# Instructions in the engines' main bodies instead of a block

## Chip, core and metric

The kernel runs on one core of a Trainium2 chip. The metric is the device time of one execution in microseconds; the time of a kernel is the median of several executions. A core has five engines, each with its own instruction stream: TensorE (PE; its weight loads are listed apart as PEld), VectorE (DVE), ScalarE (ACT), GpSimd (POOL) and SyncE (SP). [...] In the profile, a "q" behind an engine's name means its sequencer: the part that waits, jumps, drains and issues transfers.

## The reference

`x` is (1, 2048, 512) in bf16. A token mixer with a residual is followed by an MLP with a residual:

```python
def reference(x, w1, w2, w3, w4):
    h = _gelu(_layernorm(x, axis=-1) @ w1)
    ...                       # four quarters of h, shifted by 1, -1, 2, -2 tokens: g0..g3
    hs = jnp.concatenate([g0, g1, g2, g3], axis=-1) @ w2
    x1 = x + hs
    h2 = _gelu(_layernorm(x1, axis=-1) @ w3) @ w4
    return x1 + h2
```

`w1` and `w2` are 512 x 512, `w3` is 512 x 1792 and `w4` is 1792 x 512.

## The kernel before

The kernel describes its work as a list of operations, each with its engine, what it reads and what it writes. A small scheduler puts them into one order (`prog.seq`). Then `emit` writes them, with the needed waits, into the engines' instruction streams. The operations that the text speaks of:

```python
# loads of x: SyncE, and half of tile 0 on ScalarE        (lines 292, 296)
yield pg.add(eng, f"dma_x{t0}",
             lambda e: e.dma_start(x_sb[:, t0:t1, :], xt[:, t0:t1, :]), ...)
# zeros on VectorE, and matmuls on them that warm TensorE  (lines 269, 535)
pg.add("dve", "zeros", lambda e: e.memset(zeros[:], 0.0), ...)
ins = e.matmul(o_ps[:, b, :], zeros[:, 0:P], zeros[:], start=True, stop=True)
# the last stage: matmul with w4, add x1, store            (lines 511, 519, 522)
ins = e.matmul(dst, h2T[:, fc, P * t : P * (t + 1)], w4_sb[:, fc, cs], ...)
pg.add("dve", f"res{t}_{hh}", ... e.tensor_tensor(o_sb[:, oi, c], d, x1_sb[:, t, c], ALU.add) ...)
pg.add("sp", f"out_dma{t}_{hh}", ... e.dma_start(outt[:, t, c], o_sb[:, oi, c]) ...)
```

`emit` opens a block, notes the body that the block has for each engine, and writes each operation into that body. Behind the last operation SyncE waits for all 18 output transfers:

```python
    with nc.Block() as block:                                # line 593
        bodies = {}
        def keep(name):
            def _body(e):
                bodies[name] = nc.cur_body
            return _body
        block.gpsimd(keep("pool"))
        block.sync(keep("sp"))
        ...                                                  # scalar, vector, tensor
        for op in prog.seq:
            ...                                              # which semaphores it needs
            with nc.body(bodies[e]):
                ...
                engs[e].wait_ge(sems[s], v)                  # line 635
                ...
                ins = op.fn(engs[e])
                ins.then_inc(sems[op.stream], inc)
            ...
        with nc.body(bodies["sp"]):
            for op in prog.seq:
                if op.name.startswith("out_dma"):
                    nc.sync.wait_ge(sems[op.stream], 16)     # line 655
```

A program of this kind begins in a main body, which holds a few constants and one all-engine barrier (line 669 in the profile). From there each engine jumps to its own body of the block. At the block's end each engine jumps to a common end, where it drains and goes through a second all-engine barrier. In such a barrier each engine drains and adds to a semaphore, GpSimd collects four of these and adds to a second semaphore, and each engine waits for that one.

Of the kernel before, what the change touches and what calls it, by code (L numbers as in the profile page):

```python
# [12 lines left out]
ENGINES = ["sp", "act", "pe", "dve", "pool"]  # L13
# [191 lines left out]
def bass_standalone__mixer_s_mlp__prompt_kernel(nc, x, w1, w2, w3, w4, out):  # L205
# [14 lines left out]
    with ExitStack() as es:  # L220
# [356 lines left out]
        pg.line(queue)  # L577
        pg.order()
        emit(nc, es, pg)

def emit(nc, es, prog):

    engs = {"sp": nc.sync, "act": nc.scalar, "pe": nc.tensor, "dve": nc.vector, "pool": nc.gpsimd}
    sems = {e: es.enter_context(nc.semaphore("sem_" + e)) for e in ENGINES}
    ndma = 0
    for op in prog.seq:
        if op.queue is not None:
            op.stream = ("dma", ndma)
            sems[op.stream] = es.enter_context(nc.semaphore(f"sem_dma{ndma}"))
            ndma += 1  # L590
        else:
            op.stream = op.eng
    with nc.Block() as block:
        bodies = {}

        def keep(name):
            def _body(e):
                bodies[name] = nc.cur_body

            return _body  # L600

        block.gpsimd(keep("pool"))
        block.sync(keep("sp"))
        block.scalar(keep("act"))
        block.vector(keep("dve"))
        block.tensor(keep("pe"))
        know = {e: {} for e in ENGINES}
        implied = {}
        count = {}
        last_write, readers = {}, {}  # L610
        for op in prog.seq:
            e = op.eng
            needs = {}

            def need(sv):
                if needs.get(sv[0], 0) < sv[1]:
                    needs[sv[0]] = sv[1]

            for res, ver in op.reads:
                lw = last_write[res]  # L620
                assert lw[2] == ver, (op.name, res, ver, lw)
                need(lw)
            for res, ver in op.writes:
                if res in last_write:
                    need(last_write[res])
                for sv in readers.get(res, ()):
                    need(sv)
            if e == "pe":
                needs.pop("pe", None)
            k = know[e]  # L630
            with nc.body(bodies[e]):
                for s, v in sorted(needs.items(), key=lambda sv: -sv[1]):
                    if k.get(s, 0) >= v:
                        continue
                    engs[e].wait_ge(sems[s], v)
                    for s2, v2 in implied[(s, v)].items():
                        if v2 > k.get(s2, 0):
                            k[s2] = v2
                    k[s] = max(k.get(s, 0), v)
                ins = op.fn(engs[e])  # L640
                inc = 1 if op.queue is None else 16
                ins.then_inc(sems[op.stream], inc)
            val = count[op.stream] = count.get(op.stream, 0) + inc
            snap = dict(k)
            snap[op.stream] = max(snap.get(op.stream, 0), val)
            implied[(op.stream, val)] = snap
            for res, ver in op.reads:
                readers.setdefault(res, []).append((op.stream, val))
            for res, ver in op.writes:
                last_write[res] = (op.stream, val, ver)  # L650
                readers[res] = []
        with nc.body(bodies["sp"]):
            for op in prog.seq:
                if op.name.startswith("out_dma"):
                    nc.sync.wait_ge(sems[op.stream], 16)


# [26 lines left out]
```

## Time and profile before

| | |
|---|---|
| three timed executions | 139.0, 139.03 and 138.16 us, median 139.0 |
| profiled execution | 137.98 us |
| span, first to last instruction | 136.1 us |
| granted TensorE clock | 1.00 |
| instructions on record | 2007 |

The span is what the records of one execution cover, from the first instruction to the last; the device time is somewhat longer. The profile's parts that matter here are the table of busy times, the chain of work that ended last (followed back from the end, at each step to what released it), and the rows of single source lines, with the sequencers' instructions. Busy time counts only an engine's own work, so jumps, drains and barriers have to be looked for in the rows of the lines that made them: 669 for the main body, 593 for the block, 655 for the waits for outputs.

### The profile page before, as it was taken

The numbers are of one execution on the slowest core, as the hardware profiler recorded it, in microseconds if no ns is written. First come the engines' busy times: TensorE is split into PE (matmuls) and PEld (weight loads), VectorE is DVE, ScalarE is ACT, GpSimd is POOL, SyncE is SP. The second block draws the span as 40 slices with busy tenths as digits, with TensorE's granted clock in tenths as the row PEclk, the third lists the DMA queues.
The fourth block names the chain that finished last, engine by engine and source line by source line (L and its number), as shares of the span: only waits on it lengthen the run. The fifth ranks groups of instructions, "written<-read, shape, count | busy, mean of one in ns | idle before, by whom it ended". The sixth has DMA issues, their size and how long they took to land.

```text
span 136.1 us, 2007 instructions
## 1 busy us (share of the span) xinstructions
PE 130.8 (96%) x787; PEld 73.4 (54%) x800; DVE 59.0 (43%) x170; ACT 51.3 (38%) x70; POOL 19.4 (14%) x43
## 2 busy tenths in 40 slices
PE   6799999999999999999999999999999999999993
PEld 2287788776668644444444444444444444444472
DVE  1888899998899640043610053210002222322231
ACT  4899657444566455530066630036660000000000
POOL 2441483333043310001010010000000000000000
PEclk9999999999999999999999999999999999999999
DMA  3999975574379551001210003110000111111121
GB/s 104 279 371 406 357 236 102 106 90 79 70 206 174 99 113 39 0 0 39 82 39 0 0 0 76 39 39 5 0 0 30 47 39 39 43 39 39 40 72 45
DMA packets 21401, 12.19 MB, mean 90 GB/s; under 512 B 13840, under 2 KB 20880, under 8 KB 21392
## 3 DMA queue, kind: packets, MB, share of 16 engines
q1 hardware_dynamic: 21248, 12.00, 33.4%
q8 instruction: 6, 0.10, 0.3%
q10 hardware_dynamic: 144, 0.07, 0.2%
q14 instruction: 3, 0.02, 0.1%
HBM read 6.82 MB, written 2.10 MB: 65 GB/s over the span
## 4 chain that ended last, share of the span: by engine, by line
PE 85%; DVE 5%; POOL 3%; DMA 2%; issue 1%; SPq 1%; ACT 0%
PE y_ps L442 40%; PE o_ps L511 35%; PE o_ps L482 9%; POOL rstd L366 3%; DMA x_sb<-in_x_dram 2%; DVE xn_buf L372 1%; DVE st L349 1%; PE y_ps L415 1%; DVE x_sb L493 1%; POOL xn_buf L383 1%; SPq L296 1%; DVE x_sb L489 1%; DVE mv L351 0%; DVE st6b L343 0%; DVE vpe L355 0%
## 5 line engine op out<-in xcount | busy, mean ns | idle before, releaser
L442 PE MATMUL y_ps<-xnT,w_sb 128*128 128x256 bf16 (+2 forms) x435 | 64.1, 305 | 0.3
L442 PEld LDWEIGHTS y_ps<-xnT,w_sb 128*128 128x128 bf16 x440 | 40.4, 98 | 23.7 <-issue 0.4
L511 PE MATMUL o_ps<-w_sb,h2T 128*128 128x512 bf16 (+2 forms) x250 | 48.8, 355 | 0.1
L457 ACT ACTIVATE h2T<-y_ps 128x1024 bf16<-128x1024 f32 (+1 forms) x29 | 28.6, 993 | 36.6 <-PE y_ps L442 36.6
L511 PEld LDWEIGHTS o_ps<-w_sb,h2T 128*128 128x128 bf16 x252 | 23.6, 98 | 25.2
L519 DVE TENSOR_TENSOR o_sb<-o_ps,x_sb 128x512 bf16<-128x512 f32 (+2 forms) x18 | 11.4, 632 | 44.3 <-PE o_ps L511 44.1
L366 POOL TENSOR_TENSOR rstd<-vpe,neghalf 128x1 f32<-128x1 f32 x31 | 16.9, 557 | 61.6 <-DVE vpe L355 49.6
L493 DVE TENSOR_TENSOR x_sb<-o_ps,x_sb 128x512 bf16<-128x512 f32 x14 | 9.6, 689 | 22.2 <-PE o_ps L482 22.2
L349 DVE BATCH_NORM_STATS2 st<-x_sb 128x6 f32<-128x512 bf16 x26 | 17.5, 684 | 2.2 <-DMA x_sb<-in_x_dram 2.0
L482 PE MATMUL o_ps<-w_sb,hT 128*128 128x512 bf16 x58 | 15.0, 379 | 0.3
L372 DVE TENSOR_SCALAR xn_buf<-x_sb,mv,rstd 128x512 bf16<-128x512 bf16 x25 | 10.2, 411 | 3.8 <-POOL rstd L366 2.8
L457 ACT ACTIVATE hT<-y_ps 128x1024 bf16<-128x1024 f32 (+1 forms) x10 | 8.4, 850 | 7.7 <-PE y_ps L442 7.6
L482 PEld LDWEIGHTS o_ps<-w_sb,hT 128*128 128x128 bf16 x64 | 6.1, 98 | 5.3
L535 PE MATMUL o_ps<-zeros 128*128 128x512 bf16 x12 | 4.3, 534 | 1.2 <-DVE zeros L269 1.2
L380 ACT ACTIVATE xn_buf<-x_sb,nmr,rstd 128x512 bf16<-128x512 bf16 x5 | 4.0, 809 | 2.6 <-DVE nmr L376 2.6
L351 DVE BATCH_NORM_AGGREGATE mv<-st 128x2 f32<-128x6 f32 x26 | 4.1, 173 | 0.2
L355 DVE TENSOR_SCALAR vpe<-mv 128x1 f32<-128x1 f32 x26 | 3.5, 148 | 0.3
L324 ACT ACTIVATE junk<-x_sb 128x512 bf16<-128x512 bf16 x5 | 3.1, 628 | 0.7 <-DVE x_sb L489 0.7
L535 PEld LDWEIGHTS o_ps<-zeros 128*128 128x128 bf16 x12 | 1.5, 131 | 3.5 <-issue 2.1
L415 PE MATMUL y_ps<-ident,xn_buf 128*128 128x128 bf16 x28 | 2.4, 220 | 1.0 <-DVE xn_buf L372 0.9
L415 PEld LDWEIGHTS y_ps<-ident,xn_buf 128*128 128x128 bf16 x28 | 1.8, 98 | 2.1 <-DVE xn_buf L372 1.6
L420 ACT ACTIVATE xnT<-y_ps 128x512 bf16<-128x512 bf16 (+1 forms) x5 | 2.6, 548 | 0.1
(33 smaller groups left out, 18.8 us busy)
## 6 DMA issues: line engine op xcount, KB each, us to landing
out_dram<-o_sb SPq DMA_DIRECT2D x15, 128.0 KB, 1.7
w_sb<-in_w_dram SPq DMA_DIRECT2D x1, 1792.0 KB, 9.8
w_sb<-in_w_dram SPq DMA_DIRECT2D x2, 896.0 KB, 9.4
x_sb<-in_x_dram SPq DMA_DIRECT2D x2, 512.0 KB, 11.2
x_sb<-in_x_dram SPq DMA_DIRECT2D x2, 256.0 KB, 4.4
w_sb<-in_w_dram SPq DMA_DIRECT2D x2, 256.0 KB, 3.7
w_sb<-in_w_dram SPq DMA_DIRECT2D x1, 512.0 KB, 5.5
x_sb<-in_x_dram SPq DMA_DIRECT2D x3, 128.0 KB, 2.4
```

The costliest lines, as they stand in the source:

```text
L349: pg.add("dve", f"bnst{q}", lambda e: e.bn_stats(st6[:, q, :], src), reads=rs, writes=[(("st6", q), 0)], dur=605)
L351: pg.add("dve", f"bnag{q}", lambda e: e.bn_aggr(mv[:, q, :], st6[:, q, :]), reads=[(("st6", q), 0)], writes=[(("mv", q), 0)], dur=75)
L366: lambda e: e.tensor_tensor(col(rstd), col(vpe), neghalf[:], ALU.pow),
L372: lambda e: e.tensor_scalar(dst, src, mv[:, q, 0:1], rstd[:, q : q + 1], ALU.subtract, ALU.mult),
L415: ins = e.transpose(chunk(c), xn_buf[:, slot(q), P * c : P * (c + 1)], ident[:])
L442: ins = e.matmul(y_ps[:, p, W * i : W * (i + 1)], wsb[:, dc, P * fc : P * (fc + 1)], src[:, dc, P * t0 : P * t0 + W], start=(dc == 0), sto ...
L457: (lambda d, s: (lambda e: e.activation(d, s, ACT_F.Gelu_apprx_tanh)))(dst, ysrc),
L482: ins = e.matmul(dst, hT[:, j, c0 : c0 + P], w2_sb[:, j, :], start=(j == 0), stop=(j == DC - 1))
L493: f = lambda e: e.tensor_tensor(x1_sb[:, t, :], dst, x_sb[:, t, :], ALU.add)
L511: ins = e.matmul(dst, h2T[:, fc, P * t : P * (t + 1)], w4_sb[:, fc, cs], start=(fc == 0), stop=(fc == FC - 1))
L519: (lambda d, c: (lambda e: e.tensor_tensor(o_sb[:, oi, c], d, x1_sb[:, t, c], ALU.add)))(dst, cs),
L535: ins = e.matmul(o_ps[:, b, :], zeros[:, 0:P], zeros[:], start=True, stop=True)
```

## The change

The block goes. The operations are written straight into the main body, into each engine's stream, directly behind the barrier that the main body has anyway. So there is no jump into a block, none out of it, and no drain and barrier at its end. Operations, their order and their semaphores are the same; the rest of the diff is indentation.

```diff
-    with nc.Block() as block:
-        bodies = {}
-
-        def keep(name):
-            def _body(e):
-                bodies[name] = nc.cur_body
-
-            return _body
-
-        block.gpsimd(keep("pool"))
-        block.sync(keep("sp"))
-        block.scalar(keep("act"))
-        block.vector(keep("dve"))
-        block.tensor(keep("pe"))
-        know = {e: {} for e in ENGINES}
+    know = {e: {} for e in ENGINES}
 ...
-            with nc.body(bodies[e]):
-                for s, v in sorted(needs.items(), key=lambda sv: -sv[1]):
 ...
-                    engs[e].wait_ge(sems[s], v)
 ...
-                ins = op.fn(engs[e])
-                inc = 1 if op.queue is None else 16
-                ins.then_inc(sems[op.stream], inc)
+        for s, v in sorted(needs.items(), key=lambda sv: -sv[1]):
 ...
+            engs[e].wait_ge(sems[s], v)
 ...
+        ins = op.fn(engs[e])
+        inc = 1 if op.queue is None else 16
+        ins.then_inc(sems[op.stream], inc)
 ...
-        with nc.body(bodies["sp"]):
-            for op in prog.seq:
-                if op.name.startswith("out_dma"):
-                    nc.sync.wait_ge(sems[op.stream], 16)
+    for op in prog.seq:
+        if op.name.startswith("out_dma"):
+            nc.sync.wait_ge(sems[op.stream], 16)
```

More of the change, by code (lines that the diff above doesn't have):

```diff
@@ L592, in emit @@
             op.stream = op.eng
-    with nc.Block() as block:
-        bodies = {}
-        def keep(name):
-            def _body(e):
-                bodies[name] = nc.cur_body
-            return _body
-        block.gpsimd(keep("pool"))
-        block.sync(keep("sp"))
-        block.scalar(keep("act"))
-        block.vector(keep("dve"))
-        block.tensor(keep("pe"))
-        know = {e: {} for e in ENGINES}
-        implied = {}
-        count = {}
-        last_write, readers = {}, {}
-        for op in prog.seq:
[L612 to L630, printed above, removed]
-            with nc.body(bodies[e]):
-                for s, v in sorted(needs.items(), key=lambda sv: -sv[1]):
-                    if k.get(s, 0) >= v:
-                        continue
-                    engs[e].wait_ge(sems[s], v)
[L636 to L639, printed above, removed]
-                ins = op.fn(engs[e])
-                inc = 1 if op.queue is None else 16
-                ins.then_inc(sems[op.stream], inc)
[L643 to L651, printed above, removed]
-        with nc.body(bodies["sp"]):
-            for op in prog.seq:
-                if op.name.startswith("out_dma"):
-                    nc.sync.wait_ge(sems[op.stream], 16)
@@ new lines, in emit, with need @@
+    know = {e: {} for e in ENGINES}
+    implied = {}
+    count = {}
+    last_write, readers = {}, {}
+    for op in prog.seq:
+        e = op.eng
+        needs = {}
+        def need(sv):
+            if needs.get(sv[0], 0) < sv[1]:
+                needs[sv[0]] = sv[1]
+        for res, ver in op.reads:
+            lw = last_write[res]
+            assert lw[2] == ver, (op.name, res, ver, lw)
+            need(lw)
+        for res, ver in op.writes:
+            if res in last_write:
+                need(last_write[res])
+            for sv in readers.get(res, ()):
+                need(sv)
+        if e == "pe":
+            needs.pop("pe", None)
+        k = know[e]
+        for s, v in sorted(needs.items(), key=lambda sv: -sv[1]):
+            if k.get(s, 0) >= v:
+                continue
+            engs[e].wait_ge(sems[s], v)
+            for s2, v2 in implied[(s, v)].items():
+                if v2 > k.get(s2, 0):
+                    k[s2] = v2
+            k[s] = max(k.get(s, 0), v)
+        ins = op.fn(engs[e])
+        inc = 1 if op.queue is None else 16
+        ins.then_inc(sems[op.stream], inc)
+        val = count[op.stream] = count.get(op.stream, 0) + inc
+        snap = dict(k)
+        snap[op.stream] = max(snap.get(op.stream, 0), val)
+        implied[(op.stream, val)] = snap
+        for res, ver in op.reads:
+            readers.setdefault(res, []).append((op.stream, val))
+        for res, ver in op.writes:
+            last_write[res] = (op.stream, val, ver)
+            readers[res] = []
@@ L659 @@
+    for op in prog.seq:
+        if op.name.startswith("out_dma"):
+            nc.sync.wait_ge(sems[op.stream], 16)
 _INS = ['x', 'w1', 'w2', 'w3', 'w4']
```

## The prediction

> **What bounds the kernel now.** I read the busy table first, then the chain of waits, then the two ends of the run, because the change touches nothing but the two ends.
>
> ```profile
> PE 130.8 (96%) x787; PEld 73.4 (54%) x800; DVE 59.0 (43%) x170; ACT 51.3 (38%) x70; POOL 19.4 (14%) x43
> PE 85%; DVE 5%; POOL 3%; DMA 2%; issue 1%; SPq 1%; ACT 0%
> ```
>
> The first line is each engine's busy time, the second the shares of the chain that ended last. TensorE is busy for 130.8 of 136.1 us, and the chain lies on it for 85% of the span. A table of windows that I took over the span puts 125.40 us of that into the 126.25 us from 7.75 to 134.00 us. So the middle has no hole that a few instructions fewer could close. What is left is the head (0 to 7.75 us) and the tail (134.0 to 136.1 us).
>
> The head, from the chain in order of time (start, length, what held it):
>
> ```profile
> 0.65 0.07 issue
> 0.72 0.40 SPq L296
> 1.12 0.07 issue
> 1.19 0.42 SPq L296
> 1.61 0.05 issue
> 1.66 2.82 DMA x_sb<-in_x_dram
> ```
>
> SyncE leaves the first all-engine barrier at 0.65 us and issues its first load at 0.72; the next loads follow at 1.19 and 1.66, and the chain runs on through the transfer that is under way until 4.48 us. In this head the jump to SyncE's own block must lie within the 0.07 us between 0.65 and 0.72. The very next step, from one load to another with no jump in it, also takes 0.07 us. That is the first thing to see: the entry jump is nearly free here.
>
> The tail, first from the chain, in the window from 125 us on:
>
> ```profile
> 124.91 8.93 PE o_ps L511 x69
> 133.85 0.02 issue
> 133.87 0.29 DVE o_sb L519
> ```
>
> The last matmul ends at 133.85 and the last addition, which adds the residual, at 134.16 us. The chain counts computation only, so everything behind 134.16 has to be taken from the sequencers' own records. Line 655 is the loop in which SyncE waits for the output transfers; line 593 is the block itself, that is, what is behind its end. Columns: operation, count, shortest/median/longest ns, first and last start in us.
>
> ```profile
> L655 SPq EVENT_SEMAPHORE  x9: 17/28/28, 134.6 to 135.7; - x9
> ```
>
> ```profile
> L593 POOLq EVENT_SEMAPHORE  x2: 17/17/17, 136.0 to 136.0; - x2
> ...
> L593 PEldq DRAIN  x1: 1033/1033/1033, 132.8 to 132.8; - x1
> L593 DVEq DRAIN  x1: 330/330/330, 133.9 to 133.9; - x1
> L593 SPq COMPARE_BRANCH  x1: 33/33/33, 135.8 to 135.8; - x1
> L593 SPq DRAIN  x1: 13/13/13, 135.9 to 135.9; - x1
> L593 SPq EVENT_SEMAPHORE  x1: 17/17/17, 136.1 to 136.1; - x1
> ...
> L593 PEldq EVENT_SEMAPHORE  x1: 51/51/51, 136.1 to 136.1; - x1
> ```
>
> The other engines had reached the end long before (TensorE's drain starts at 132.8, VectorE's at 133.9). They wait at the barrier for SyncE, which waits for the last output transfer. From 135.7 to the end of the span at 136.1 us nothing is done but jump, drain and barrier.
>
> [...] The trace has only one jump on record at all, SyncE's at the end, with 33 ns, and 130 ns pass between it and the next instruction; for the other engines' jumps and for all five entry jumps it has none[...]. [...] the profiled execution took 137.98 us for a span of 136.14, so 1.84 us lie outside the records.
>
> **The change, part by part.** Compared engine by engine, both programs have the same work in the same order with the same waits; each engine loses four instructions (GpSimd five): a jump in, a jump out, a drain, and one wait on the barrier's semaphore (two semaphore operations on GpSimd, which collects and releases). The barrier ahead of the work stays. So there are three terms.
>
> 1. The entry jumps. SyncE's step from barrier to first load is 0.07 us, as is its step from load to load. ScalarE goes from the end of its barrier wait to its own load in 56 ns by the records. Nothing there has the size of a further stop. VectorE takes 172 ns to its memset of the zeros, and a jump may be in that; but the memset only starts the warm-up matmuls, and their row (L535) ends near 5.5 us, while TensorE's first transpose waits until 6.34 us for normalised data from the loads. On the path: 0.00 to 0.05 us; I take 0.02.
>
> 2. The exit on SyncE, the only one on the path. The records in nanoseconds: last wait for an output ends at 135.716; 37 to the jump's start; 33 for the jump; 130 until the drain; 13 for it; 25 until GpSimd sees it; 17 + 62 + 17 for GpSimd's two operations; 36 until the last engine reads the release; 51 for TensorE's operation on it. The sum is 421 ns and reaches the end of the span, 136.137. All of it goes: 0.42 us.
>
> 3. The waits for the outputs. There are 18 semaphores. Before, nine operations of line 655 take 17 and the jump carries the eighteenth; after, nine operations carry two each. The first eight start 0.06 us apart, at 134.57 to 135.01 us, all behind the last issue (134.19 to 134.52) and all ahead of the landing of that last transfer at 135.69, for which the ninth waits. So the repacking is hidden by 0.65 us: 0.00 us.
>
> Sum: 0.42 + 0.02 = 0.44 us of 136.14, that is 0.3%. The new span should be 135.7 us. The 1.84 us outside the records I leave as they are, minus perhaps 0.1 us, since four engines now come early to whatever stands behind the kernel; I chose this share, nothing shows it.
>
> **The rivals.**
>
> First, the **barrier's time is not saved but moved**[...]. For this speaks that SyncE comes last in any case and the last landing at 135.69 us doesn't move. [...] the time would stay at that of before, 138.5 to 139.0 us, with a shorter span.
>
> Second, the **entry jumps cost more than I see**[...]. Were all of it on the path, another 0.1 us would come off. The chain says otherwise: it goes over SyncE's loads, and neither memset nor warm-up is in it.
>
> Third, a **shifted start changes the transfers**: loads that start 0.02 us earlier could meet in another order in the queues, and TensorE at 96% busy would feel only a missed due time in the first 8 us. I see no cause for more than 0.1 or 0.2 us either way, as all loads move together.
>
> Fourth, **the scatter hides it all**: the three timed runs of before are 139.0, 139.03 and 138.16 us, and the profiled one 137.98. The gap between the two pairs, some 0.9 us, is twice the expected gain. A median of few runs can land on either.
>
> **Range and chances.** The median of before, 139.0, less 0.45 gives 138.55; the mean of all four executions, 138.54, less 0.45 gives 138.1. I choose 138.3 between the two. The range takes half a microsecond and a little more on each side for the scatter: 137.98 less 0.45 is 137.5 as the low end, and 139.0, the old median with no gain at all, as the high end. Faster by over 2% would need 2.8 us, more than the whole tail of 2.3 us behind the last matmul; slower by 2% would need an unforeseen stall of as much. So 0.02 and 0.01, and 0.97 for within 2%.
>
> **What would show it right or wrong.** Right: the rows of the block's end (drain, jump, barrier) are gone; the last record is SyncE's ninth wait for outputs; the span is 135.6 to 135.8 us; SyncE's first load starts 0.07 us behind the barrier as before; the chain's shares are the same. Step 1 is wrong if the first load or the memset of the zeros moves by more than 0.05 us and the first transpose with it. Step 2 is wrong if the tail from the last addition to the end doesn't shrink from 1.98 to about 1.55 us. The share outside the records is wrong if execution less span is no longer near 1.8 us. The prediction as a whole is wrong if the middle changes: another busy time of TensorE, or a granted clock below the 1.00 of now.

## The result and the profile after

Six executions of the changed kernel have a median of 137.27 us (136.93 to 138.08); six of the kernel before, beside them, have 138.93 us (138.09 to 139.30). The ratio is 0.9898, with a 95% interval of 0.9856 to 0.9941. So it is faster by about 1%, within the 2% to which the prediction gave 0.97, but by more than the predicted 0.3%; 137.27 also lies 0.2 us below the low end of the range, 137.5.

The profiled execution took 137.32 us for a span of 135.99 us. The page's busy table and the engine shares of the chain:

```profile
PE 131.5 (97%) x787; PEld 73.6 (54%) x800; DVE 58.9 (43%) x170; ACT 51.3 (38%) x70; POOL 19.4 (14%) x43
PE 85%; DVE 5%; POOL 3%; DMA 2%; issue 1%; SPq 1%; ACT 0%
```

The same work and the same chain, then, at the same granted clock of 1.00. The 0.7 us more on TensorE are the twelve warm-up matmuls (4.3 us before, 5.0 after), which are not on the chain: one takes 0.63 us at first and 0.38 at the end, and the short ones start at 4.45 us before and at 5.83 after. The head of the chain after (start, length, what held it):

```profile
0.66 0.07 issue
0.72 0.40 SPq L296
1.12 0.06 issue
1.18 0.43 SPq L296
1.61 0.05 issue
1.66 3.10 DMA x_sb<-in_x_dram
```

SyncE's first load still starts at 0.72 us. Its step from the barrier to the load is 68 ns in both kernels by the records, and VectorE's to its memset 172 before and 171 after: the entry jumps cost these two nothing. What differs is the transfer: 3.10 us instead of 2.82. The copy below takes up whether that is the block's doing. The end of the chain, and SyncE's waits for the outputs (now line 639):

```profile
124.98 9.15 PE o_ps L511 x70
134.13 0.02 issue
134.16 0.29 DVE o_sb L519
```

```profile
L639 SPq EVENT_SEMAPHORE  x9: 28/28/28, 134.9 to 136.0; - x9
```

The ninth wait, which starts at 135.96 and ends at 135.987 us, is the last record. Nothing stands on the block's line any more. Laid side by side from the records, in ns:

| stretch | before | after |
|---|---|---|
| start to second half of tile 0's statistics (needs the chain's load) | 4501 | 4785 |
| from there to the end of the last addition | 129661 | 129660 |
| last addition to the end of the span | 1975 | 1542 |
| device time less span (us) | 1.84 | 1.33 |

The middle is the same to a nanosecond. The tail lost 0.43 us, as predicted; the later load in this one execution gave 0.28 of it back, so the span fell by only 0.15 us. And the part outside the records fell by 0.51 us. That last row was not foreseen, and the experiments are about it.

### The profile page after: what moved, and what is told of

Its sections match the earlier page's. It is cut to its first block, busy times and chain, and to the rows that moved or that the text cites. A ratio compares the mean times of both kernels' runs of the same rounds, so it can differ in the third digit from the quotient of the medians.

```text
span 136.0 us, 1995 instructions
## 1 busy us (share of the span) xinstructions
PE 131.5 (97%) x787; PEld 73.6 (54%) x800; DVE 58.9 (43%) x170; ACT 51.3 (38%) x70; POOL 19.4 (14%) x43
## 4 chain that ended last, share of the span: by engine, by line
PE 85%; DVE 5%; POOL 3%; DMA 2%; issue 1%; SPq 1%; ACT 0%
PE y_ps L442 40%; PE o_ps L511 36%; PE o_ps L482 9%; POOL rstd L366 3%; DMA x_sb<-in_x_dram 2%; DVE xn_buf L372 1%; DVE st L349 1%; PE y_ps L415 1%; DVE x_sb L493 1%; POOL xn_buf L383 1%; SPq L296 1%; DVE x_sb L489 1%; DVE mv L351 0%; DVE st6b L343 0%; DVE vpe L355 0%
## 5 line engine op out<-in xcount | busy, mean ns | idle before, releaser
L535 PE MATMUL o_ps<-zeros 128*128 128x512 bf16 x12 | 5.0, 606 | 1.2 <-DVE zeros L269 1.2
```

## Experiments

Each kernel was timed beside the kernel before on the same chip. For each the time outside the records is given: device time less span, as the median of the 9 to 22 executions of that experiment. It holds what lies ahead of the first record together with what lies behind the last, and nothing here divides the two; differences between kernels are put down to the end, as the part ahead of the work is the same. It scatters by only +-0.07 us, far less than the times themselves, and +-0.05 of that is rounding, since the spans of these executions are on record to 0.1 us. The one profiled execution of each kernel, with a span to the nanosecond, gives the same values within 0.04 us. In the kernel before it was 1.82 or 1.83 us on every chip (27 to 57 executions).

### The changed kernel once more

> The changed kernel once more, unchanged. In the first profiles the tail behind the last addition shrank by 0.43 us and the time outside the records (device time less span) from 1.84 to 1.33, together 0.94 us or a ratio of 0.993; the measured ratio was 0.990. Theory of scatter (the first load of x lands at another time in each execution, and the rest is chance): spans from 135.5 to 137 us, outside 1.33 +- 0.05 in each execution, and a ratio that comes nearer to 0.993. Rival (the head is systematically faster without the block): the ratio stays at 0.990 or below, and the first tile's loads land earlier than in the kernel before.

Median 137.77 us against 138.29, ratio 0.9945 (0.9923 to 0.9967). Outside 1.37 us (mean 1.355), so 0.46 less than before. Together with the 0.42 us of jump, drain and barrier this makes 0.88 us, 0.64% of 138.3, a ratio of 0.9936; that lies within the intervals of both comparisons. The shortest executions agree: 137.17 against 138.04, 0.87 us. The ratio moved towards the sum, as the theory of scatter had it, and the head is not faster (second half of tile 0's statistics at 4.82 us). Nor is it slower as a rule, though the profiles alone could suggest it: those statistics start at 4.50 us in before and 4.62 in the other kernel below that keeps the block, and at 4.63 to 5.12 in the twelve without it. But the lower group of spans lies around 136.3 us for before and around 135.9 for the copy, 0.4 us apart, which is the exit alone. This profile also scatters in another place than I had put it: its middle is 130.45 us, not 129.66. That is taken up after the experiments.

### The barrier alone

> The changed kernel with one all-engine barrier put back behind the last wait, without block and jump. By the records of before, jump and the step behind it were 0.20 us of the tail, drain and barrier 0.22. Theory of late arrival (each engine has something to finish behind its last instruction, and the barrier lets four engines begin with it only when the last transfer has landed): tail 1.75 to 1.8 us, outside back at 1.8, so some 0.7 us above the changed kernel. Rival [...]: outside stays at 1.33, time 0.2 us above the changed kernel.

```diff
+    nc.all_engine_barrier()          # behind the last wait, in the main body
```

Rows of that line (operation, count, shortest/median/longest ns, first and last start):

```profile
L640 POOLq EVENT_SEMAPHORE  x2: 17/17/17, 136.8 to 136.9; - x2
L640 POOLq DRAIN  x1: 651/651/651, 82.3 to 82.3; - x1
...
L640 SPq DRAIN  x1: 7/7/7, 136.8 to 136.8; - x1
...
L640 PEldq EVENT_SEMAPHORE  x1: 51/51/51, 137.0 to 137.0; - x1
```

Median 138.24 us, ratio 0.9994 (0.9969 to 1.002), by the two ratios 0.68 us above the changed kernel, where 0.7 was expected; outside 1.83 us. From the last wait to the end of the span 0.25 us, where the kernel before had 0.42. So the barrier alone brings the whole time outside back, and 0.25 of the 0.42 us; the jump with the step behind it is the other 0.17. The rival, that the jump costs the time outside, is out. GpSimd's drain at 82.3 us shows that the engine had finished long ago and was only held by the barrier.

### All engines late, without a barrier

> The changed kernel, with one wait added at the end of each of the other four engines, for the last output transfer: no barrier, no drain, no jump, but all five engines reach their end together. Theory of late arrival: outside goes back to about 1.8 us, span as in the changed kernel (at most 0.05 more), time 0.5 us above it. Rival (barrier, drain or jump themselves cost the time outside): outside 1.33, time as the changed kernel.

```diff
+    last = [op for op in prog.seq if op.name.startswith("out_dma")][-1]
+    for e in ("act", "pe", "dve", "pool"):
+        engs[e].wait_ge(sems[last.stream], 16)
```

```profile
L642 ACTq EVENT_SEMAPHORE  x1: 17/17/17, 135.9 to 135.9; - x1
L642 POOLq EVENT_SEMAPHORE  x1: 17/17/17, 135.9 to 135.9; - x1
L642 DVEq EVENT_SEMAPHORE  x1: 21/21/21, 135.9 to 135.9; - x1
L642 PEldq EVENT_SEMAPHORE  x1: 51/51/51, 135.9 to 135.9; - x1
```

No drain, no barrier and no jump, yet outside is 1.86 us (ratio 0.9986, 0.9968 to 1.0004). So the time outside comes not from those instructions, but from engines that reach their end late.

### One engine late at a time

In these four the 18 waits for the outputs are moved to one other engine, and SyncE ends at its last issue:

```diff
-            nc.sync.wait_ge(sems[op.stream], 16)
+            engs["pool"].wait_ge(sems[op.stream], 16)     # or "act", "dve", "pe"
```

> The changed kernel with the 18 waits for the outputs on GpSimd instead of SyncE, so SyncE ends at its last issue and GpSimd is the only late engine. Theory of late arrival: the time outside is what the late engine has to finish, so it differs from 1.33 by the difference between the two engines, up or down by 0.1 to 0.5 us. Rival (time outside belongs to barrier or jump): 1.33 as in the changed kernel.

> The changed kernel with the 18 waits for outputs on ScalarE instead of SyncE. So far the time outside the records is 1.82 us in before, 1.36 with SyncE late alone, 1.86 with all five late, 2.12 with GpSimd late alone. Theory (each engine has its own finishing work, and the end waits for all of it; GpSimd's is the longest): ScalarE between 1.2 and 1.9 us. Rival (the engines finish in a fixed order, a chain that passes from one to the next; the earlier the late engine stands in it, the longer): also between these, but the five engines give five different, evenly spaced values.

> The changed kernel with the 18 waits on VectorE. Theory of own finishing work: outside 1.2 to 1.9 us. Rival of a fixed order: a value evenly spaced between those of the other engines. If any engine comes below SyncE's 1.36 at the same span, the waits belong on that engine and the kernel beats the changed one by the difference.

> The changed kernel with the 18 waits on TensorE. TensorE's semaphore operations take 51 ns in the records where SyncE's take 17 to 28, so the span may be 0.03 us longer. Theory of own finishing work: outside 1.2 to 1.9 us. Rival of a fixed order: evenly spaced values.

| engine that is late alone | outside, us | ratio (95%) |
|---|---|---|
| SyncE (changed kernel, the copy) | 1.37 | 0.9945 (0.9923 to 0.9967) |
| VectorE | 1.42 | 0.9944 (0.9916 to 0.9972) |
| ScalarE | 1.47 | 0.993 (0.9901 to 0.9959) |
| TensorE | 1.57 | 0.9949 (0.9925 to 0.9972) |
| GpSimd | 2.12 | 1.001 (0.9987 to 1.0033) |

The time outside depends on which engine is late, and for GpSimd it is the longest by far. The values are not evenly spaced (0.05, 0.05, 0.10, 0.55; the last is 0.33 with GpSimd's 1.90 for a single wait, below), so a fixed chain with equal steps doesn't fit. A chain with unequal steps, which passes from engine to engine, is not ruled out: it too would give each late engine a value of its own. GpSimd late alone, with all the waits on it, takes away the whole gain. No engine comes below SyncE: the changed kernel already waits on the cheapest one. The differences in time between the first four are smaller than their intervals; only the time outside tells them apart.

### GpSimd beside SyncE, GpSimd left out, GpSimd with one wait

> The changed kernel (SyncE waits for all outputs) with one wait for the last output on GpSimd as well. With all five late the time outside was 1.86 us, with GpSimd late alone 2.12. Theory (GpSimd's finishing work sets the end, and its nine operations at the end made it worse alone): 1.85 to 1.9 us here, which is the value of before, so GpSimd alone explains the whole 0.46 us. Rival (it takes several late engines to get 1.86): between 1.36 and 1.8. Third (a late GpSimd is worse when the others are early): 2.1.

> All five engines late gave 1.86 us outside the records, GpSimd with SyncE 1.90; ScalarE, VectorE and TensorE late alone gave 1.47, 1.42 and 1.57. Here all but GpSimd wait for the last output. Theory (the slowest of the late engines sets the time outside, and that is GpSimd): without it TensorE sets it, 1.5 to 1.6 us. Rival (it is the number of late engines): about 1.75, between one late and five.

> GpSimd late alone gave 2.12 us, but it then had nine operations with 18 waits at its end; with SyncE late too, and one wait on GpSimd, it was 1.90. Here SyncE waits for the first 17 outputs and GpSimd only for the last. Theory (the longer list of waits on GpSimd costs the 0.22 us): 1.90 us. Rival (a late GpSimd is worse when SyncE is early): 2.1 us.

```diff
 # pool_late_too: SyncE's waits stay
+    nc.gpsimd.wait_ge(sems[last.stream], 16)
 # four_late: as all engines late, but with: for e in ("act", "pe", "dve")
 # pool_last_only: SyncE waits for outs[:-1], and then
+    nc.gpsimd.wait_ge(sems[outs[-1].stream], 16)
```

Outside: 1.90 us with GpSimd late beside SyncE, 1.61 with the four others late and GpSimd early, 1.90 with one wait on GpSimd and SyncE early. The ratios are 0.9959 (0.9937 to 0.9981), 0.9959 (0.9944 to 0.9974) and 0.9994 (0.9974 to 1.0013). The first and the third are alike outside and still lie 0.0035 apart, so the scatter of the times hides what tells the three apart. The late engine with the largest value sets the time, not their number: without GpSimd it is near TensorE's 1.57. A chain with unequal steps would do the same. And of GpSimd's 2.12, 0.22 us belonged to its nine operations of waits:

```profile
L639 POOLq EVENT_SEMAPHORE  x9: 43/43/43, 119.0 to 136.5; - x9
```

```profile
L640 POOLq EVENT_SEMAPHORE  x1: 17/17/17, 136.8 to 136.8; - x1
```

The first line is of the kernel with all waits on GpSimd, the second of the one with the last alone. Why nine operations, eight of which were over before, cost 0.22 us behind the ninth stays open.

### The block's barrier in its other form

> The kernel before, with the block's closing barrier in its other form, without GpSimd's drain and with semaphores alone. GpSimd still leaves last, behind the landing of the last output. Theory of the late GpSimd: outside 1.8 to 1.9 us as in before, and at most the 0.25 us of the barrier change in the tail. Rival (the drain on GpSimd is what costs outside the records): outside 1.4 us.

```diff
-    with nc.Block() as block:
+    with nc.Block(no_gpsimd_drain=True) as block:
```

Outside 1.81 us, ratio 1.0021 (0.9992 to 1.005). So GpSimd's drain is not what costs the time outside, and this form gains nothing: GpSimd still ends only behind the last landing. The other four engines still drain in it, and SyncE's exit takes 0.49 us instead of 0.42, with one semaphore operation more.

This gives one number for six kernels. GpSimd's last record ends before the span does, by 0.087 us in before (136.050 against 136.137), 0.09 in the barrier alone and in this one, 0.04 with all late and 0.00 in the two with a single wait on GpSimd. Added to the time outside of 1.82, 1.83, 1.81, 1.86, 1.90 and 1.90, it comes to 1.90 to 1.92 us each time from GpSimd's last record to the end of the execution, with what lies ahead of the first record counted in.

### The last wait alone on SyncE

> On GpSimd nine operations of waits at the end instead of one cost 0.22 us outside the records (2.12 against 1.90). SyncE, the engine whose late end is the cheapest, carries such a list in the changed kernel. Here ScalarE waits for the first 17 outputs, which land 0.7 us earlier, and SyncE for the last alone. Theory (the list costs any engine the same): outside 1.1 to 1.2 instead of 1.36, and a kernel 0.2 us below the changed one. Rival (the list matters on GpSimd alone): 1.36, time as the changed kernel.

```diff
-    for op in prog.seq:
-        if op.name.startswith("out_dma"):
-            nc.sync.wait_ge(sems[op.stream], 16)
+    outs = [op for op in prog.seq if op.name.startswith("out_dma")]
+    for op in outs[:-1]:
+        nc.scalar.wait_ge(sems[op.stream], 16)
+    nc.sync.wait_ge(sems[outs[-1].stream], 16)
```

Outside 1.34 us, ratio 0.9941 (0.9918 to 0.9964): no gain that can be measured. The list of waits matters on GpSimd and not on SyncE, and the theory falls. No kernel that I tried is measurably faster than the changed one.

### Where the scatter is

From the second half of tile 0's statistics to the end of the last addition, the fourteen profiles fall into groups: 129.66 us in five (before and after among them), 130.30 to 130.50 in eight (the copy among them), 130.03 in one. The transposing transfers, line 389, in after and then in the copy:

```profile
L389 SPq DMA_TRANSPOSE xnT<-xn_buf x24: 1190/1264/1852, 19.2 to 82.6; - x24
```

```profile
L389 SPq DMA_TRANSPOSE xnT<-xn_buf x24: 1189/1265/2322, 19.3 to 83.5; - x24
```

In the copy one of them, issued at 27.2 us, held SyncE for 2.32 instead of 1.27 us. TensorE waits not for that one but for the one issued before it, at 25.86 us, which takes 4.12 us to land (most take 2.5). From the chain and from the waits of the copy:

```profile
25.86 4.12 DMA xnT<-xn_buf
29.98 0.14 issue
30.12 1.91 PE y_ps L442 x16
```

```profile
PE y_ps L442 <- DMA xnT<-xn_buf: 0.6, 1, 0.6
```

After's chain stays on TensorE from 19.98 us throughout that stretch. What goes with it is a 16 KB transfer on queue q8, whose kind the profile gives as instruction. It starts at 26.6 to 27.2 us in all eight profiles of the long kind, at 29.1 to 29.9 in the five short ones, and at 31.4 in the one between, which has its long transpose issue at 30.7. In both kinds it falls upon a transposed transfer; what differs is which. In the copy it starts 1.08 us behind the issue at 25.86, whose transfer TensorE soon needs, and is still under way when SyncE issues the next. In after it starts 1.07 us behind the issue at 28.38. That transfer lands late too, after 3.6 us, but the next issue comes only at 30.53 us and keeps its 1.19 us, and the chain doesn't wait for it. From issue to landing, for the transposes of after in the window from 28.3 to 30 us:

```profile
DMA to landing us min/median/max: 2.5/3.1/3.6
```

All fourteen profiles together have 336 transpose issues. The 23 that take 1.77 to 2.34 us all have such a q8 transfer under way; the other 313 take at most 1.37 us. After's 1.85 us is one of fourteen near 42 us, one in every profile, so these don't tell the groups apart. DMA queues in the window from 26.5 to 28.5 us, first of after, then of the copy:

```profile
q1 hardware_dynamic: 663, 0.16, 39.9%
```

```profile
q1 hardware_dynamic: 529, 0.12, 70.9%
q8 instruction: 1, 0.02, 4.7%
```

In the copy the q8 transfer is in this window, and the transposes' fewer packets (529 against 663) take a larger share of the engines' time. That goes together in every profile; that the q8 transfer is the cause was not tested, and why its start varies stays open. The kernel before shows both kinds too: its 57 executions beside the copy have spans that crowd around 136.3 us, with a second group around 137.0.

## Why the prediction was right, and where it was wrong

**The bound and the rivals on the head: right.** The middle didn't change, and the entry jump costs SyncE 0 ns (68 and 68). My 0.02 us for it should have been 0.00. The second rival, an entry jump that costs VectorE or TensorE more, falls with VectorE's 172 and 171 ns and with TensorE's first instruction at 1.17 us in both kernels.

**The exit, 0.42 us: right.** The tail went from 1.975 to 1.542 us, to the "about 1.55" given as the test. The experiment with the barrier alone divides the 0.42 us into 0.25 for drain and barrier and 0.17 for the jump and the step behind it; by the records of before I would have said 0.22 and 0.20, and the difference is the 0.04 us step behind the last wait, which the barrier needs as well. One reading beside it was loose: the chain does not count computation alone, since SyncE's issues and a transfer are in its head; it just ends with the last addition.

**The repacked waits, 0.00 us: right.** Nine operations with two waits each; the eighth ends at 135.33 us, 0.63 ahead of the ninth's start.

**The term that was mis-sized is the 1.84 us outside the records**, "as they are, minus perhaps 0.1 us". It fell by 0.46 (1.82 to 1.37). The direction was there, and its tie to the four engines that now come early, but I gave it a size by choice. What the runs show in its place is that the late engine with the largest value sets the size: GpSimd's 1.90 us from its last record, of which 1.82 lay outside the span in before, and SyncE's 1.37 once it alone is late (each with what lies ahead of the first record). With it the sum is 0.42 + 0.46 = 0.88 instead of 0.44 us, 0.64% instead of 0.3%.

**The first rival, that the barrier's time is only moved, fell the other way:** the time outside shrank, from 1.82 to 1.37 us. The runs show the effect of lateness engine by engine; what the engines do in that time no record shows.

**The fourth rival, the scatter, was real, and it is why the first comparison went beyond 0.88 us.** Device time less 1.82 us puts four of the first six executions of before at spans of 137.0 us or more, in the upper group; of the changed kernel's six only one, with 136.8, was. Three of six at some 0.8 us (130.45 less 129.66) make 0.4 us of the mean. That is reckoned from spans, as those executions left no trace. With 0.88 it comes to 1.3 us, and 1.0% of 138.9 is 1.4. This and the 0.36 us missing in the mis-sized term put the median below the range.

## What to carry to other kernels

An engine that has finished should be let go: in this kernel an all-engine barrier at the end cost 0.25 us within the span and 0.46 us outside it, because it kept GpSimd until the last transfer had landed. A late GpSimd cost 0.5 us more than a late SyncE, so one engine alone, SyncE, should wait for the outputs. And where a change touches a kernel's ends, compare device time less span as well as the times: here it scatters by 0.07 us where the two groups of spans lie 0.8 us apart.

## What the hardware showed that I had not expected

- The time outside the records goes by which engine ends late: with that engine late alone, SyncE 1.37 us, VectorE 1.42, ScalarE 1.47, TensorE 1.57, GpSimd 1.90 with one wait and 2.12 with nine operations of waits.
- Four of the five engines' exit jumps leave no record in the kernel before; SyncE's, a COMPARE_BRANCH that carries a wait, takes 33 ns and is followed by 130 ns in which SyncE records nothing.
- A transposing transfer's issue mostly takes 1.27 us and its landing 2.5 us. Where a 16 KB transfer on the instruction queue, q8, fell at its time, the issue took up to 2.3 us and the landing, in the copy, up to 5.1. In the eight profiles where that happened at 27 us, the middle was 0.64 to 0.84 us longer.
